# Another order for the first batch of a packed-attention and gated-FFN kernel, with the two elementwise steps of softmax 2 swapped between VectorE and GpSimd

## The chip, the core and the metric

The kernel runs on one core of one Trainium2 chip. The metric is device time in microseconds of one execution. A core has TensorE (PE in the profile; its weight loads stand apart as PEld), VectorE (DVE), ScalarE (ACT), GpSimd (POOL) and SyncE (SP), which issues every load and store of this kernel. Each engine runs its own list of instructions strictly in the order written, and waits where a semaphore tells it to.

## What is computed

The reference is attention of a small packed set of queries, attention of the full queries on its result, and a gated feed-forward net without a nonlinearity:

```python
def sm_attn(qq, kk, vv):
    s = scale * np.matmul(qq, kk.transpose(0, 1, 3, 2))
    s = s - np.max(s, axis=-1, keepdims=True)
    a = np.exp(s)
    a = a / (np.sum(a, axis=-1, keepdims=True) + 1e-09)
    return np.matmul(a, vv)
p_packed = sm_attn(p, k, v)             # p: 8 x 8 heads x 32 x 64; k, v: 8 x 8 x 576 x 64
out = sm_attn(q, p_packed, p_packed)    # softmax 2: rows of 32
x = out as (8 * 576) tokens x 512
y = ((x @ w_a) * (x @ w_b)) @ w_out     # w_a, w_b: 512 x 1536, w_out: 1536 x 512
```

The three weight matrices arrive in 64-bit floating point, everything else in 32 bits. The output is float32.

## The kernel before

The work goes batch by batch (`for b in range(B)`, 8 batches of 576 tokens and 8 heads). The heads are split in two halves, e = 0 and e = 1, four heads each.

**Attention of a batch.** `stage1(b, e)` makes the packed attention of one half: scores (L247), maximum (L253), exponential on ScalarE (L257), transposes on TensorE (L271, L272), product with v (L281), and the scaled result `pp` (L287). `turned` turns `pp` into `ppT` (L236, L237). `stage2(b, e)` is the second attention: scores (L297), then softmax 2 on a tile `s2`: a transpose to 32-wide rows (L302), maximum (L304), subtraction of the maximum (L307), exponential (L309), sum and reciprocal (L312 to L314), multiplication by the reciprocal (L315), a transpose back (L318), and a split into a rounded high part `a2_hi` (L319, ScalarE) and a low part `a2_lo` (L322, which the profile shows at the helper's line L86). L307 and L315 run on the engine that the variable `eng` holds. In the profile `s2` of batch 0 is called s, later ones t, and the parts a_hi and a_lo.

**FFN of a batch.** The second attention's product with the packed values is not formed by itself: `g_tiles(b, c)` multiplies `ppT` with a 512-wide piece of `w_ab` (L332), and `mm1` multiplies that with the softmax parts. `g_tiles` also splits its result into `ghi` (ScalarE, L338) and `glo` (VectorE, shown at L86). One call serves two of the twelve steps `ft` of `mm1`. A step makes two products with three passes each (high with high, high with low, low with high), 12 matmuls of 288 columns a half (L351): the first goes into one pair of PSUM banks (`pa`), ScalarE copies it to `asb` (L363), the second goes into the other pair (`pb`), and VectorE multiplies the two (L366). There are two pairs: the next step's first product waits for L363, its second for L366. ScalarE and GpSimd then split the gated result into `h_hi` (L370) and `h_lo` (L86). After twelve steps `mm2_part` (L377) multiplies with `wo_hi` and `wo_lo`, three passes again. For batch 0 it goes through the first nine slices of `w_out` for all four token tiles, one slice after the other, so that slices can be converted late.

**Weight conversion**, in batch 0 alone. 36 pieces of 512 KB are loaded (`raw`, 12 buffers) and turned into 32 bits by three steps, each run in order of the pieces: A (`high_word`, ScalarE, L189), B (`low_word`, on ScalarE at L197, or on VectorE or GpSimd at L194, as the table `WAYS` says with 0, 1 or 2), and C (`both_words`, VectorE, L200), after which the buffer is free and the next piece is loaded. Pieces 4c to 4c + 3 are what `g_tiles` needs for c; pieces 24 to 35 are `w_out`, and for these C writes a single buffer, `wo_f32`, which step D (`split_wout`) rounds on ScalarE (L225) and subtracts on GpSimd (L86, tile wo).

**What sets the order.** All five engines follow the written order (`manual_schedule`). Three tables of short names write it for batch 0: `FIRST` the loads (p, k, q, v in parts, w a weight piece; part 0 and 1 are heads 0 to 3 and 4 to 7, part 2 the last 64 tokens of all heads), `START` all steps before the first `mm1`, and `PLAN_0`, whose slots are emitted one after each half of an `mm1` step and between the groups of `mm2`. In them T and P are `turned`, k and q the transposes of loaded keys and queries, S0 and S1 the start of `stage1`, r its further steps for each half, s0 and s1 the steps of `stage2`, g the first `g_tiles`, L a load for a later batch, A to D conversion steps. `TURN` says which engine copies each transposed piece of batch 0 out of PSUM (0 VectorE, 1 ScalarE; five for k, five for q). `PLAN` is the same for the later batches.

Of the kernel before, what the change touches and what calls it, by code (L numbers as in the profile page):

```python
# [19 lines left out]
def tile_packed_attn_gated_ffn(  # L20
# [20 lines left out]
    nc = tc.nc  # L41
    B, H, S, D = q.shape
# [42 lines left out]
    def lo_part(dst, src, hi, eng=nc.vector):  # L85
        return eng.tensor_tensor(out=dst, in0=src, in1=hi.bitcast(F32), op=ALU.subtract)  # L86

    def bank():
        return ps_x.tile([P, 512], F32, name="x")

    def bank_pair(s=False):
        return ps_s.tile([P, 2, 512], F32, name="s") if s else ps_m.tile([P, 2, 512], F32, name="m")

    def work(b, name, shape, tag=None):
        if b == 0:
            return scratch.tile(shape, F32, name=name)
        return wk.tile(shape, F32, name=tag, bufs=2 if tag == "t1" else 1)
# [82 lines left out]
    def xT_cols(b, key, u, h, cols=slice(0, HS)):  # L180
        return xTs[b, key][h // R][64 * u:64 * u + 64, h % R, cols]
# [108 lines left out]
    def stage2(b, e):  # L290

        TU = 2 * XH
        hi, lo = (t[:, e, :].rearrange("p (x u l) -> p u x l", u=2, l=TL) for t in (a2_hi, a2_lo))
        x = bank_pair(b == 1 or e == 0)
        for r in range(R):
            for u in range(2):
                nc.tensor.matmul(  # L297
                    out=x[J * r:J * r + J, u, 0:HS], lhsT=ppT[64 * u:64 * u + 64, 1 if u ^ e else 2 * (b % 2), r, :],
                    rhs=xT_cols(b, "q", u, 2 * r + e), start=True, stop=True)
        yield  # L300
        s2 = work(b, f"s2_{e}", [P, TU, J], "t1")
        nc.vector.transpose(out=s2.rearrange("p (u x) j -> p u (x j)", u=2), in_=x[:, :, 0:HS])  # L302
        mx = sm.tile([P, TU], F32, name="mx")
        nc.vector.tensor_reduce(out=mx, in_=s2, axis=AX, op=ALU.max)  # L304
        yield
        eng = nc.gpsimd if b or e else nc.vector
        eng.tensor_tensor(out=s2, in0=s2, in1=mx.unsqueeze(2).broadcast_to([P, TU, J]), op=ALU.subtract)  # L307
        yield
        nc.scalar.activation(out=s2, in_=s2, func=AF.Exp, scale=scale)  # L309
        yield  # L310
        sum2 = sm.tile([P, TU], F32, name="sum2")
        nc.vector.tensor_reduce(out=sum2, in_=s2, axis=AX, op=ALU.add)  # L312
        nc.vector.tensor_scalar(out=sum2, in0=sum2, scalar1=1e-9, scalar2=None, op0=ALU.add)
        nc.vector.reciprocal(out=sum2, in_=sum2)  # L314
        eng.tensor_tensor(out=s2, in0=s2, in1=sum2.unsqueeze(2).broadcast_to([P, TU, J]), op=ALU.mult)  # L315
        yield
        a2f = work(b, f"a2f_{e}", [P, 2, XH, TL], "t2")
        nc.vector.transpose(out=a2f.rearrange("p u x l -> p (u x l)"), in_=s2.rearrange("p x j -> p (x j)"))  # L318
        nc.scalar.copy(out=hi, in_=a2f)  # L319
        yield  # L320
        lo_part(lo, a2f, hi)
        yield  # L322
# [97 lines left out]
    def emit(b, plan, tasks={}):  # L420

        for name in plan.split():
# [30 lines left out]
            elif what == "Lp":  # L453
# [1 line left out]

    st = {}

    FIRST = ("p0 k0 k1 k2 q2 q0 v0 q1 v1 w1 w1 w1 w1 w1 w1 w1 w1 w1 w1 w1")
    START = ("T0 k0 k4 k1 k3 k2 q0 S0 S1 r0 q1 r1 r1 r0 r0 r1 r0 q2 r1 q3 P0 q4 A s0 A B s0 s0 B s1 s0 B s1 A s1 "
             "s0 C B Lp2 A C s1 s1 B A B B C B A C A s0 s1 s0 C Lk2 C B g A Lv2 A A C A B C B s1 C B A B Lk3 C A "  # L460
             "s1")
    WAYS = ("000000022220202120112012011200110102")
    TURN = ("1001111101")

    PLAN = (" | S0 | r0 |  | r0 | r0 |  | r0 Lv1 |  | S1 | r1 | q0 Lk2 | r1 |  |  | r1 q1 Lk3 |  | r1 Lv2 |  |  | "
            "T2 P0 |  |  | s0 s0 s1 g s0 |  | s1 | Lp4 s0 s1 s1 k2 | s0 | s0 | s1 s0 | s1 Lq2 | s1 | k3 Lq3")
    PLAN = dict(enumerate(PLAN.split("|")))
    PLAN_0 = ("B | C C | C A B A | C C A B B | A C A | k0 | A | B Lq0 B B | B C A C T0 A | C Lp2 C k1 | B A A | S0 "
# [3 lines left out]
    PLAN_0 = dict(enumerate(PLAN_0.split("|")))  # L472

    pieces = [(c, n) for c in range(NC) for n in range(4)] + [(NC, f) for f in range(NFT)]
# [12 lines left out]
    def convert(x):  # L487
# [14 lines left out]
        elif x == "B":  # L502
            low_word(raw, int(WAYS[pieces.index((c, n))]))
        else:
# [17 lines left out]
    ep(tc.manual_schedule(engines={ET.PE, ET.DVE, ET.Activation, ET.Pool, ET.SP}))  # L522
    for name in FIRST.split():
        what, i = name[0], int(name[1])
# [9 lines left out]
    tasks = {"g": next_g(0)}  # L534
    emit(0, START, tasks)
    drain(tasks["g"])
# [6 lines left out]
    for b in range(B):  # L543
        plan = dict(PLAN if b else PLAN_0)
        slot, tasks = [0], {"g": next_g(b + 1)}
# [73 lines left out]
```

## Time and profile before

| | |
|---|---|
| median of 3 runs | 748.11 us (747.31 to 749.12) |
| the profiled execution: its time | 747.04 us |
| the profiled execution: first to last instruction (span) | 745.3 us |
| TensorE busy, matmuls | 719.9 us, 97% of the span |
| VectorE, ScalarE, GpSimd busy | 308.8, 281.4, 214.1 us |
| read from HBM, written | 47.97 MB, 9.44 MB |

Outside the span lie 747.04 - 745.3 = 1.7 us. A busy time is the union of an engine's instructions; where TensorE is nearly always busy, what it waits for in a stretch is told by the waits and by the distance between the starts of its matmuls.

### The profile page before, as it was taken

The page shows a single profiled execution, that of the slowest core. Times are in us where ns is not written, and L with a number is a line of the kernel's source. Part 1 is how long each engine was busy: PE and PEld are TensorE (multiplying, and loading weights), DVE is VectorE, ACT ScalarE, POOL GpSimd, SP SyncE. Part 2 cuts the span into 40 slices and gives each one's busy share as a digit, 9 for nine tenths or more (in the row PEclk, how much of TensorE's full clock was granted, in tenths as well). Part 3 has the DMA queues.
Part 4 walks back from the last instruction along what each step waited for, and adds up shares of the span by engine and source line. Part 5 has one row for each costly group of instructions (what it writes and reads, how often), then busy time and mean ns, then how long its engine had stood idle before and what let it go on. Part 6 is the DMA issues. An engine that isn't in the chain of part 4 may idle for free.

```text
span 745.3 us, 13719 instructions
## 1 busy us (share of the span) xinstructions
PE 719.9 (97%) x5844; PEld 602.9 (81%) x5844; DVE 308.8 (41%) x487; ACT 281.4 (38%) x494; POOL 214.1 (29%) x155
## 2 busy tenths in 40 slices
PE   5589899999999999999999999999999999999998
PEld 4278777888888888889788897888888888888887
DVE  2898856355303553244702446045520455123200
ACT  3777743444114531344203542055311553034300
POOL 0395754334103340133301333033400334023300
PEclk9799999999999999999999999999999999999999
DMA  8999952432510414014230242314050100100011
GB/s 255 362 255 256 284 100 54 88 67 54 92 41 24 71 43 91 30 45 90 47 74 15 55 80 47 76 33 73 24 106 29 33 1 2 43 15 1 1 29 43
DMA packets 171005, 58.30 MB, mean 78 GB/s; under 512 B 140608, under 2 KB 158784, under 8 KB 170944
## 3 DMA queue, kind: packets, MB, share of 16 engines
q1 hardware_dynamic: 170944, 57.43, 31.6%
q8 instruction: 46, 0.75, 0.4%
q14 instruction: 15, 0.12, 0.0%
HBM read 47.97 MB, written 9.44 MB: 77 GB/s over the span
## 4 chain that ended last, share of the span: by engine, by line
PE 91%; DVE 3%; DMA 1%; POOL 1%; issue 1%; ACT 1%; SPq 0%; DVEq 0%; POOLq 0%; ACTq 0%
PE m L377 40%; PE m L351 39%; PE x L332 6%; PE s L281 1%; PE s L247 1%; DVE w_ab L200 1%; PE s L297 1%; DMA kn<-in_k_dram 1%; PE s L271 1%; POOL wo L86 1%; DMA raw<-in_moe_w_b_dram 1%; DVE wo_f L200 1%; PE x L236 0%; PE m L297 0%; PE m L147 0%
## 5 line engine op out<-in xcount | busy, mean ns | idle before, releaser
L377 PE MATMUL m<-wo,h_hi 128*128 128x512 f32 (+1 forms) x888 | 268.8, 385 | 0.8 <-DVE asb L366 0.8
L86 POOL TENSOR_TENSOR h_lo<-asb,h_hi 128x576 fp32r<-128x576 f32 x96 | 138.6, 1444 | 411.5 <-ACT h_hi L370 411.3
L377 PEld LDWEIGHTS m<-wo,h_hi 128*128 128x128 f32 x888 | 164.2, 188 | 40.0 <-DVE t L302 5.0
L366 DVE TENSOR_TENSOR asb<-m,asb 128x576 f32<-128x576 f32 x96 | 72.6, 756 | 279.9 <-PE m L351 277.5
L351 PE MATMUL m<-a_hi,ghi 128*128 128x288 f32 x768 | 171.0, 304 | 2.4 <-ACT asb L363 1.7
L377 PE MATMUL m<-wo,h_lo 128*128 128x512 f32 (+1 forms) x444 | 170.4, 384 | 0.0
L351 PE MATMUL m<-a_lo,ghi 128*128 128x288 f32 x768 | 163.9, 295 | 0.9 <-DVE a_lo L86 0.9
L351 PEld LDWEIGHTS m<-a_hi,ghi 128*128 128x128 f32 x768 | 122.1, 188 | 39.7 <-issue 16.8
L351 PE MATMUL m<-a_hi,glo 128*128 128x288 f32 x768 | 133.4, 295 | 1.0 <-DVE glo L86 1.0
L351 PEld LDWEIGHTS m<-a_lo,ghi 128*128 128x128 f32 x768 | 123.5, 188 | 1.1 <-DVE a_lo L86 1.1
L370 ACT CAST h_hi<-asb 128x576 fp32r<-128x576 f32 x96 | 64.7, 674 | 143.0 <-DVE asb L366 143.0
L351 PEld LDWEIGHTS m<-a_hi,glo 128*128 128x128 f32 x768 | 112.7, 188 | 1.2 <-DVE glo L86 1.2
L377 PEld LDWEIGHTS m<-wo,h_lo 128*128 128x128 f32 x444 | 83.4, 188 | 16.7
L86 DVE TENSOR_TENSOR glo<-x,ghi 128x512 fp32r<-128x512 f32 x96 | 61.7, 684 | 52.7 <-ACT ghi L338 52.7
L363 ACT COPY asb<-m 128x576 f32<-128x576 f32 x96 | 61.6, 641 | 39.2 <-PE m L351 31.5
L332 PE MATMUL x<-w_ab,ppT 64*32 64x512 f32 x768 | 57.9, 606 | 7.9 <-DVE w_ab L200 7.9
L412 ACT COPY asb<-m 128x512 f32<-128x512 f32 x24 | 14.1, 587 | 134.2 <-PE m L377 133.4
L338 ACT CAST ghi<-x 128x512 fp32r<-128x512 f32 x96 | 51.4, 588 | 5.9 <-PE x L332 5.9
L119 DVE STREAM_TRANSPOSE xT<-nat 128x1152 f32<-128x1152 f32 x28 | 38.3, 1367 | 0.0
L412 ACT COPY wo_f<-m 128x512 f32<-128x512 f32 x11 | 6.5, 588 | 55.4 <-PE m L377 55.4
L332 PEld LDWEIGHTS x<-w_ab,ppT 64*32 64x32 f32 x768 | 13.6, 106 | 15.9 <-issue 12.3
L194 POOL TENSOR_SCALAR raw<-raw 128x512 uint32<-128x512 uint32 x11 | 23.7, 2157 | 0.9
(106 smaller groups left out, 407.2 us busy)
## 6 DMA issues: line engine op xcount, KB each, us to landing
nat<-in_k_dram SPq DMA_DIRECT2D x56, 144.0 KB
nat<-in_q_dram SPq DMA_DIRECT2D x56, 144.0 KB
vt<-in_v_dram SPq DMA_DIRECT2D x28, 256.0 KB
raw<-in_moe_w_a_dram SPq DMA_DIRECT2D x12, 512.0 KB
raw<-in_moe_w_b_dram SPq DMA_DIRECT2D x12, 512.0 KB
raw<-in_moe_w_out_dram SPq DMA_DIRECT2D x12, 512.0 KB
out_dram<-asb SPq DMA_DIRECT2D x17, 256.0 KB
out_dram<-wo_f SPq DMA_DIRECT2D x10, 256.0 KB
```

Of the source, the lines that this page charges most:

```text
L86: return eng.tensor_tensor(out=dst, in0=src, in1=hi.bitcast(F32), op=ALU.subtract)
L119: nc.vector.transpose(out=xT.rearrange("p h t -> p (h t)"), in_=t.rearrange("p h x d -> p (h x d)"))
L194: (nc.vector if way == 1 else nc.gpsimd).tensor_scalar(out=low, in0=low, scalar1=2.0 ** -29, scalar2=7.0, op0=ALU.mult, op1=ALU.min)
L200: nc.vector.scalar_tensor_tensor(out=dst.bitcast(U32), in0=raw[..., 1], scalar=3, in1=raw[..., 0], op0=ALU.logical_shift_left, op1=ALU.bit ...
L332: nc.tensor.matmul(out=gps[e][J * r:J * r + J, :], lhsT=ppT[rows, 2 * (b % 2), r, :], rhs=w_ab[rows, c, r, :], start=True, stop=True)
L338: nc.scalar.copy(out=ghi[:, e], in_=gps[e])
L351: nc.tensor.matmul(out=ps[:, half, 0:HS], lhsT=gt[:, kt, i, :], rhs=at[:, kt, HS * half:HS * half + HS], start=(n == 0 and kt == 0), stop= ...
L363: nc.scalar.copy(out=asb, in_=pa[:, :, 0:HS])
L366: nc.vector.tensor_tensor(out=asb, in0=pb[:, :, 0:HS], in1=asb, op=ALU.mult)
L370: nc.scalar.copy(out=hh, in_=flat)
L377: nc.tensor.matmul(out=o[:, cols], lhsT=ht[:, c0:c0 + P], rhs=wt[:, cols], start=(ft == 0 and n == 0), stop=(ft == NFT - 1 and n == 2))
L412: nc.scalar.copy(out=ob, in_=o)
```

## The change

`stage2` of batch 0 runs L307 and L315 of half 0 on GpSimd and those of half 1 on VectorE; before it was the other way round. The table `SUBS` has one digit for each half of batches 0 and 1; for batch 1 it says GpSimd, as before. The other tables are written anew.

```diff
-        eng = nc.gpsimd if b or e else nc.vector
+        eng = nc.vector if b < 2 and SUBS[2 * b + e] == "1" else nc.gpsimd
...
-    FIRST = ("p0 k0 k1 k2 q2 q0 v0 q1 v1 w1 w1 w1 w1 w1 w1 w1 w1 w1 w1 w1")
...
+    FIRST = ("p0 k0 k2 k1 q0 v0 q1 v1 q2 w1 w1 w1 w1 w1 w1 w1 w1 w1 w1 w1")
...
-    TURN = ("1001111101")
...
+    TURN = ("0001110101")
+    SUBS = ("0100")
```

In `WAYS` five digits change: pieces 18, 30 and 33 go from VectorE to ScalarE, piece 34 from ScalarE to VectorE, piece 35 from GpSimd to ScalarE. In `START` the last part of the queries (q4) now stands ahead of P0, and the conversion steps stand elsewhere between the steps of softmax 2. In `PLAN_0` T0, the transposes of batch 1's packed queries, stand in slot 7 and not in 8, which is half a step of `mm1` earlier; T2, the same for batch 2, in slot 21 and not in 29; the conversions keep their own order and stand in other slots.

Three places on VectorE show what the tables do to an engine's list. The first is in the middle of softmax 2 of batch 0: from the last two of the first four conversions to the first gated product (L366). In both lists two conversions stand before the first row. Before:

```order
L200 SCALAR_TENSOR_TENSOR w_ab<-raw 128x2x256 x2
L318 STREAM_TRANSPOSE a2f_405<-s_0_344 128x576
L318 STREAM_TRANSPOSE a2f_408<-s_1_361 128x576
L86 TENSOR_TENSOR a_lo<-a2f_405,a_hi 128x2x9x32
L200 SCALAR_TENSOR_TENSOR w_ab<-raw 128x2x256 x2
L86 TENSOR_TENSOR glo<-x,ghi 128x512 x2
L200 SCALAR_TENSOR_TENSOR w_ab<-raw 128x2x256 x2
L86 TENSOR_TENSOR a_lo<-a2f_408,a_hi 128x2x9x32
L200 SCALAR_TENSOR_TENSOR w_ab<-raw 128x2x256 x2
L366 TENSOR_TENSOR asb<-m,asb 128x576
```

The same engine and place in the changed kernel:

```order
L200 SCALAR_TENSOR_TENSOR w_ab<-raw 128x2x256 x2
L318 STREAM_TRANSPOSE a2f_404<-s_0_352 128x576
L318 STREAM_TRANSPOSE a2f_407<-s_1_362 128x576
L200 SCALAR_TENSOR_TENSOR w_ab<-raw 128x2x256
L86 TENSOR_TENSOR a_lo<-a2f_404,a_hi 128x2x9x32
L86 TENSOR_TENSOR glo<-x,ghi 128x512 x2
L200 SCALAR_TENSOR_TENSOR w_ab<-raw 128x2x256
L86 TENSOR_TENSOR a_lo<-a2f_407,a_hi 128x2x9x32
L200 SCALAR_TENSOR_TENSOR w_ab<-raw 128x2x256 x4
L366 TENSOR_TENSOR asb<-m,asb 128x576
```

Two of the conversions that stood ahead of a_lo of half 1 stand behind it now, ahead of the first gated product.

The second place is VectorE in the steps 7 to 9 of batch 0's `mm1`, where the first slices of `w_out` are converted (wo_f is the buffer `wo_f32`). Before:

```order
L366 TENSOR_TENSOR asb<-m,asb 128x576
L200 SCALAR_TENSOR_TENSOR w_ab<-raw 128x2x256 x2
L200 SCALAR_TENSOR_TENSOR wo_f_917<-raw 128x512
L194 TENSOR_SCALAR raw<-raw 128x512
L366 TENSOR_TENSOR asb<-m,asb 128x576
L200 SCALAR_TENSOR_TENSOR wo_f_964<-raw 128x512
L194 TENSOR_SCALAR raw<-raw 128x512
L86 TENSOR_TENSOR glo<-x,ghi 128x512 x2
```

In the changed kernel:

```order
L366 TENSOR_TENSOR asb<-m,asb 128x576
L200 SCALAR_TENSOR_TENSOR w_ab<-raw 128x2x256
L200 SCALAR_TENSOR_TENSOR wo_f_935<-raw 128x512
L194 TENSOR_SCALAR raw<-raw 128x512
L260 TENSOR_SCALAR rs<-rs 128x1
L261 RECIPROCAL rs<-rs 128x1
L366 TENSOR_TENSOR asb<-m,asb 128x576
L200 SCALAR_TENSOR_TENSOR wo_f_983<-raw 128x512
L86 TENSOR_TENSOR glo<-x,ghi 128x512 x2
```

One conversion less stands ahead of the first wo_f, and `glo` follows the second wo_f without an L194 between.

The third place is VectorE at the end of `mm1` of batch 0: the last two gated products, behind which `mm2` starts. Before:

```order
L200 SCALAR_TENSOR_TENSOR wo_f_1050<-raw 128x512
L366 TENSOR_TENSOR asb<-m,asb 128x576
L287 TENSOR_SCALAR pp<-s,rs 128x64 x2
L200 SCALAR_TENSOR_TENSOR wo_f_1127<-raw 128x512
L366 TENSOR_TENSOR asb<-m,asb 128x576
L194 TENSOR_SCALAR raw<-raw 128x512
```

In the changed kernel:

```order
L200 SCALAR_TENSOR_TENSOR wo_f_1050<-raw 128x512
L366 TENSOR_TENSOR asb<-m,asb 128x576
L287 TENSOR_SCALAR pp<-s,rs 128x64 x2
L237 COPY pT<-x 128x256
L366 TENSOR_TENSOR asb<-m,asb 128x576
L119 STREAM_TRANSPOSE xT_1147<-nat_722 128x1152
```

The fifth wo_f no longer stands ahead of the last gated product; the copy of T2 stands there.

## Rows read from the trace of the kernel before

**Rows 1.** Stretches: length, busy us of each engine, clock, DMA share, GB/s.

```profile
25.00:41.25 16.25, 5.79 (x32) 2.36 (x31) 15.93 (x26) 13.09 (x24) 9.74 (x6) 0.68 0.97 334
41.25:66.00 24.75, 24.39 (x212) 19.91 (x213) 23.64 (x33) 18.04 (x32) 18.76 (x11) 1.00 0.96 258
66.00:92.68 26.68, 24.59 (x247) 21.15 (x245) 19.93 (x30) 19.79 (x37) 17.81 (x12) 1.00 0.97 268
130.00:745.30 615.30, 612.05 (x4899) 519.42 (x4897) 218.65 (x350) 204.68 (x355) 147.63 (x108) 1.00 0.22 47
```

**Rows 2.** Waits of TensorE: us in total, times, longest.

```profile
PE m L351 <- ACT asb L363: 1.7, 2, 1.3
...
PE x L152 <- DMA kn<-in_k_dram: 1.3, 1, 1.3
...
PE m L377 <- DVE asb L366: 0.8, 1, 0.8
```

**Rows 3.** Chain that ended last, 16 to 24 us: start, us, what.

```profile
16.60 0.47 ACT xT L149
...
21.72 0.63 PE x L152 x8
...
23.61 0.80 DVE s L302
```

**Rows 4.** The same chain, 25 to 42 us.

```profile
25.22 0.76 DVE s L307
...
29.82 1.20 DVE w_ab L200 x2
...
32.20 2.10 DVE w_ab L200 x2
...
36.48 1.55 DVE w_ab L200 x2
...
39.25 1.27 DVE w_ab L200 x2
...
41.25 1.58 PE m L351 x10
```

**Rows 5.** Timeline of TensorE, first `g_tiles`: start, us, instruction, wait before.

```profile
32.89 1.93 PE L332 MATMUL x<-w_ab,ppT 64*32 64x512 f32 x8 [7.88 <-DVE w_ab L200]
```

**Rows 6.** Timeline of GpSimd, softmax 2 of batch 0.

```profile
27.54 1.16 POOL L307 TENSOR_TENSOR s<-s,mx 128x576 f32<-128x576 f32 x1 [26.24 <-DVE mx L304]
32.34 1.40 POOL L315 TENSOR_TENSOR s<-s,sum 128x576 f32<-128x576 f32 x1 [3.65 <-ACT raw L189]
```

**Rows 7.** Line L200, 22 to 95 us: duration in ns, least/median/most.

```profile
L200 DVE SCALAR_TENSOR_TENSOR w_ab<-raw x24: 628/683/1783, 29.7 to 74.1; 128x512 uint32<-128x512 uint32 x24
...
L200 DVE SCALAR_TENSOR_TENSOR wo_f<-raw x5: 889/1902/1919, 74.7 to 90.1; 128x512 uint32<-128x512 uint32 x5
```

**Rows 8.** VectorE by line, 41.25 to 66 us: busy us, mean ns, idle before.

```profile
L200 DVE SCALAR_TENSOR_TENSOR w_ab<-raw 128x512 uint32<-128x512 uint32 x13 | 10.9, 856 | 0.6 <-POOL raw L194 0.4
...
L194 DVE TENSOR_SCALAR raw<-raw 128x512 uint32<-128x512 uint32 x4 | 2.8, 729 | 0.0
```

**Rows 9.** The chain again, 42 to 61 us: the `g_tiles` of c = 1 and c = 3.

```profile
42.83 1.02 PE x L332 x16
...
59.04 1.84 PE x L332 x16
```

**Rows 10.** Timelines of ScalarE and VectorE, 78 to 92 us.

```profile
80.65 0.62 ACT L225 CAST wo<-wo_f 128x512 fp32r<-128x512 f32 x1 [1.59 <-DVE wo_f L200]
...
82.13 0.65 ACT L363 COPY asb<-m 128x576 f32<-128x576 f32 x1
...
78.71 1.90 DVE L200 SCALAR_TENSOR_TENSOR wo_f<-raw 128x512 uint32<-128x512 uint32 x1 [1.11 <-POOL wo L86]
...
90.06 1.90 DVE L200 SCALAR_TENSOR_TENSOR wo_f<-raw 128x512 uint32<-128x512 uint32 x1 [1.02 <-POOL wo L86]
```

**Rows 11.** Waits of SyncE's queue, 0 to 60 us.

```profile
SPq L210 <- DVE w_ab L200: 10.4, 4, 6.7
```

More of the change, by code (lines that the diff above doesn't have):

```diff
@@ L456, in tile_packed_attn_gated_ffn @@
     st = {}
-    FIRST = ("p0 k0 k1 k2 q2 q0 v0 q1 v1 w1 w1 w1 w1 w1 w1 w1 w1 w1 w1 w1")
[L459 to L462, printed above, removed]
-    TURN = ("1001111101")
+    FIRST = ("p0 k0 k2 k1 q0 v0 q1 v1 q2 w1 w1 w1 w1 w1 w1 w1 w1 w1 w1 w1")
+    START = ("T0 k0 k4 k1 k3 k2 q0 S0 S1 r0 r1 q1 r1 r0 r0 r1 r0 q2 r1 q3 q4 P0 s0 B s1 A s0 B A A s0 s0 B s1 C A "
+             "s1 B s0 C s1 A s1 C B B Lp2 C A B A s0 s1 B C B B s0 B g A C A A s1 Lv2 Lk2 C C A A C B B Lk3 C s1")
+    WAYS = ("000000022220202120012012011200010010")
+    TURN = ("0001110101")
+    SUBS = ("0100")
     PLAN = (" | S0 | r0 |  | r0 | r0 |  | r0 Lv1 |  | S1 | r1 | q0 Lk2 | r1 |  |  | r1 q1 Lk3 |  | r1 Lv2 |  |  | "
@@ L467, in tile_packed_attn_gated_ffn @@
     PLAN = dict(enumerate(PLAN.split("|")))
-    PLAN_0 = ("B | C C | C A B A | C C A B B | A C A | k0 | A | B Lq0 B B | B C A C T0 A | C Lp2 C k1 | B A A | S0 "
[3 rows of a table removed]
+    PLAN_0 = ("A | C C | B A B A | B C C B C | A A | C | B | C B A T0 k0 Lp2 A | A A B B C Lq0 | C C k1 | A B A | "
[3 rows of a table added]
     PLAN_0 = dict(enumerate(PLAN_0.split("|")))
```

6 rows, old and new, of the table PLAN_0 are left out of this document.

## The prediction

> **What bounds the kernel now.** I read the stretches first [rows 1]. From 130 us on TensorE is busy for 612.05 of 615.30 us at the full clock, and the rest is the last copy and store: that part moves as a block, and what batch 0 ends earlier or later is what the kernel gains or loses. Nothing of the change lies behind batch 0's mm2. So I ask only where TensorE stands before its first L377.
>
> There are two such parts. From 25 to 41.25 us it is busy for 5.79 of 16.25 us, at a mean clock of 0.68, while VectorE is busy for 15.93 [rows 1]: the chain runs through VectorE's queue, from softmax 2 (L302, 23.61) to the a_lo of half 1, behind which the second part of the first mm1 step starts at 41.25 [rows 3, 4]. These 17.64 us are VectorE's list, one instruction behind the other. From 41.25 to the first L377 TensorE is nearly full, with three waits: two for L363, 1.3 the longest of 1.7 in all, and 0.8 for L366 at the start of mm2 [rows 2]. A fourth is hidden in a busy row: the g_tiles of c = 3 holds the chain for 1.84 us, that of c = 1 for 1.02 [rows 9].
>
> **The change, part by part.**
>
> *Loads of batch 0, up to softmax 2.* The transposes of k stop for 1.3 us until the third part of k lands, which was loaded behind the second [rows 2]. Now it is loaded ahead of it; together the parts are as large as before, so the second lands when the third did. The transposes of the third fill that wait, and scores and first maximum come 1.3 us earlier. I take 1.2, because part of this work then runs while the clock is still low. Less if another load is late: bound 0 to 1.5. Behind that, two edits cancel by my reading: a copy of q leaves ScalarE ahead of half 1's exponential, -0.47, and the eight transposes of q4 now stand ahead of P0, on the path to ppT, +0.63, of which the copy of q3 on VectorE, which waits there anyway, hides a little [rows 3]. Softmax 2 thus starts at 23.61 - 1.2 = 22.4. **-1.2.**
>
> *Softmax 2, the engines swapped.* VectorE has as many subtractions and products as before, for the other half. On GpSimd they take 1.16 and 1.40 [rows 6], on VectorE 0.76 the subtraction, and I take the same for the product [rows 4]: 1.0 longer for half 0. I cost this at nothing: while GpSimd works, VectorE does the transpose and maximum of half 1, a conversion and its subtraction, and later half 1's sums and product; the transpose back of half 0 (L318) stands behind all that. Without this cover it costs up to 1.0.
>
> *VectorE's list from 22.4 on.* In before, eight conversions (L200) stand ahead of a_lo of half 1, in four pairs of 1.20, 2.10, 1.55 and 1.27 [rows 4]; now six. The two that go are half of the last two pairs: (1.55 + 1.27) / 2 = 1.4. The second pair is 0.9 longer than the first; the trace shows GpSimd's L315 from 32.34 on beside it [rows 4, 6]. Now L315 starts before that pair, beside one conversion and sums, and I take the 0.9 as gone. Against this, VectorE will reach glo before ghi is there. The first g_tiles starts behind the third conversion, and ahead of that stand the same steps in both lists: at 32.89 - 23.61 = 9.3 us into the list, at most a little earlier. Its first eight matmuls take 1.93 at the low clock [rows 5], all sixteen, overlapped, some 3.5; with the cast (0.6) ghi of half 0 is there at 13.4. VectorE ends the fourth conversion at 34.30 - 23.61 - 0.9 = 9.8; two transposes (1.5), a conversion (0.6) and a_lo of half 0 (0.7) later it is ready, at 12.6. So it waits 0.8. Sum -1.4 - 0.9 + 0.8 = **-1.5**, and the mm1 run that started at 41.25 starts at 41.25 - 1.2 - 1.5 = 38.55. Bounds: -0.6 (the 0.9 is only moved) to -2.3 (no wait for ghi).
>
> *What moves into the next stretch.* From 41.25 to 66 VectorE is busy for 23.64 of 24.75 us [rows 1]. The two conversions come back here, 2 x 0.683 [rows 7], less one low-word step of 0.73 that WAYS and the later slots take out of it [rows 8]: +0.6. The copy for T0, which held up the g_tiles of c = 3 by 1.84 - 1.02 = 0.8 [rows 9], now stands behind fewer conversions on VectorE, and T0 half a step earlier on TensorE: -0.8. **-0.2.** Bounds: -1.0 to +1.4. GpSimd starts on its low words about 4 us earlier, since its L315 no longer comes at 32.34, and the SP queue gets buffers back earlier: 10.4 us of its waits up to 60 us are for L200 [rows 11]. So I see no new wait for a piece.
>
> *The w_out conversions.* The 1.3 wait comes from a ping-pong over one buffer: L200 into wo_f takes a median of 1.90, against 0.68 for the same work into w_ab [rows 7]; L225 waits 1.59 for it, the casts of ghi and the copy L363 stand behind L225 on ScalarE, and the copy comes at 82.13 [rows 10]. In the new list the first wo_f stands one conversion earlier and starts before that step's h_lo on GpSimd, so that the second wo_f starts in a pause of GpSimd. By the rows laid end to end from 38.55 on, L363 comes only some 0.2 us before TensorE needs it, so I count on it, with a rival below: **-1.3**, bound 0 to -1.5. At the end of mm1 the last L366 stood behind a wo_f of 1.90 (90.06) [rows 10]; now a copy of T2 stands there, ready long before: **-0.8**, bound 0 to -0.9.
>
> The narrow rows are the ones where a VectorE instruction runs beside GpSimd: 1.78 against 0.68, 1.90 against 0.68 [rows 7]. The Trainium skill (SBUF — State Buffer, Who interferes with whom) states a lock: a VectorE instruction with two SBUF inputs and a GpSimd one that reads SBUF exclude each other, and the one that starts second waits until the first has ended. The rows agree, with up to 1.2 us a time. By this rule the gain of the wo_f part hangs on who starts first, which is the second rival below.
>
> Sum: -1.2 - 1.5 - 0.2 - 1.3 - 0.8 = -5.0. The profiled execution took 747.04, so 742.0; it lies 1.07 below the median of the runs, 748.11, to which I hold the forecast: **743.1 us**.
>
> **Rivals.**
>
> *The list of VectorE becomes the bound, and it is slower.* Place: 38 to 62 us, where VectorE has two conversions more, TensorE comes earlier, and GpSimd is busy for 18.76 of 24.75 [rows 1]. For it: 95% busy before, and a conversion there took 0.856 on average, 0.17 over its median [rows 7, 8]. Against it: L366 has most of a half step of slack, and GpSimd's low words come earlier. Price: 14 conversions stand there; at m us each they add 14 x (m - 0.856). The gain of 5.0 is used up at m = 1.21, and at 1.35, if nearly all stand behind a GpSimd instruction, the time is 748.1 - 5.0 + 6.9 = 750.0. Chance 0.08.
>
> *The waits on the w_out side stay.* The lock falls the other way, the ping-pong over wo_f keeps its pace, and the 1.3 and 0.8 are paid again: 743.1 + 2.1 = 745.2. For it: the margin of 0.2, and five wo_f of which the median is a blocked one [rows 7]. Against it: one conversion less in front, and no wo_f at all ahead of the last L366. Chance 0.22.
>
> *The loads bind, and there is little or no change.* The DMA share is 0.96 to 0.97 from 25 to 92.68 [rows 1]. If pieces land when they did, what TensorE gains at the start it waits for later, and only the two waits of the first part of mm1 and a little of the start remain: 748.1 - 1.0 = 747.1. Against it: 10.4 us of SP's waits are for buffers, not for landings [rows 11], and no row of TensorE's waits behind the first 10 us names a load [rows 2]. Chance 0.11.
>
> **How the numbers follow.** The forecast's own case, all five terms within their bounds and not all at one end, has 0.59 and reaches from 741.1 to 745. With the second rival (about 744 to 746.5) and most of the third this gives a range of 741.1 to 747.4, which leaves out the slower rival, the end of the third and the best ends of the terms. A change of 0.2%, 1.5 us, is about what a measurement of this kernel tells from none. Faster by more than that (below 746.6): 0.59 + 0.22 + a small part of the third, 0.81; within: 0.10; slower (above 749.6): 0.09, the first rival and some that I did not think of.
>
> **What would show it.** Right: the first L302 near 22.4, and the second part of the first mm1 step near 38.6; the wait of L152 for k gone; the g_tiles of c = 3 as short as the others; no wait of TensorE over 0.5 us between 60 us and the first L377, which comes some 4 us earlier, and behind it no 0.8; everything from batch 1 on the same, some 5 us earlier. Wrong: waits of L351 for L366 or glo between 38 and 62 us with conversions of over 1 us in front of them (first rival); L225 waiting over 1 us ahead of ghi near 75 us (second); L351, L332 or VectorE waiting for raw or nat (third). The clock is a common risk: if it comes back later than 37 us, the first products run at half speed, and 0.1 us a matmul is lost for as long.

## The result, and the profile after

The changed kernel takes 741.73 us (median of 4 runs, 740.84 to 741.94), the kernel before 747.93 us beside it (4 runs): a ratio of 0.9913, 95% interval 0.9896 to 0.9930, so 6.2 us less where 5.0 were forecast. Of the two profiled executions, on which the forecast was built, the span falls from 745.3 to 740.2 us, by 5.1.

First the stretches of the changed kernel (columns as in [rows 1]): to the g_tiles of c = 1, from there to 66 us, to the first L377, and the rest.

```profile
25.00:41.11 16.11, 8.12 (x48) 5.95 (x55) 15.84 (x26) 13.02 (x23) 12.88 (x7) 0.58 0.99 345
41.11:66.00 24.89, 24.89 (x234) 20.54 (x234) 21.83 (x33) 20.07 (x36) 17.17 (x11) 1.00 1.02 277
66.00:86.39 20.39, 20.39 (x220) 18.61 (x213) 15.96 (x27) 16.84 (x30) 16.22 (x11) 1.00 0.98 266
125.00:740.20 615.20, 611.95 (x4898) 519.35 (x4896) 219.27 (x350) 204.56 (x355) 147.57 (x108) 1.00 0.22 47
```

These are not quite the cuts of [rows 1]: there 41.25 lies inside the first step of `mm1`, and 92.68 is the fourth L377. To the g_tiles of c = 1, the first stretch of before is:

```profile
25.00:42.76 17.76, 7.30 (x42) 3.71 (x41) 17.44 (x27) 13.86 (x26) 11.25 (x6) 0.71 0.98 321
```

The last row of the changed kernel is that of before: the rest moved as a block. In its two middle rows TensorE never stands. In the first it is busy longer than before, 8.12 against 7.30 us, at a lower mean clock, 0.58 against 0.71. Its waits, that answer to [rows 2]:

```profile
PE x L332 <- DVE w_ab L200: 8.1, 1, 8.1
...
PE x L147 <- DMA kn<-in_k_dram: 2.9, 1, 2.9
...
PE m L351 <- ACT ghi L338: 0.7, 1, 0.7
...
PE s L281 <- DMA vt<-in_v_dram: 0.3, 1, 0.3
```

The waits for L363 and L366 are gone, and that of L152 for the third part of k; so are two of before that stood inside the first step of `mm1`:

```profile
PE m L351 <- DVE glo L86: 1.0, 1, 1.0
PE m L351 <- DVE a_lo L86: 0.9, 1, 0.9
```

One is longer: the first L147 waits 2.9 for the first part of k, 1.6 before. One is new, for vt, the loaded v of batch 1, in the first part of `mm2`. The chain, at the places of [rows 3, 4, 9] (the chain counts a group from the end of what stood before it, so it starts up to 0.1 later than in a timeline):

```profile
23.17 0.80 DVE s L302
...
32.30 2.51 PE x L332 x16
35.43 5.68 PE m L351 x24
41.11 1.02 PE x L332 x16
...
56.73 1.02 PE x L332 x16
```

L302 comes 0.44 earlier, not 1.2. From 35.43 to 41.11 the chain runs through TensorE and no longer through VectorE's list. The timeline of TensorE shows why that step is so long:

```profile
35.43 0.85 PE L351 MATMUL m<-a_hi,ghi 128*128 128x288 f32 x2 [0.69 <-ACT ghi L338]
...
39.44 0.68 PE L351 MATMUL m<-a_hi,glo 128*128 128x288 f32 x2
...
40.69 0.42 PE L351 MATMUL m<-a_hi,glo 128*128 128x288 f32 x2
...
78.22 0.42 PE L351 MATMUL m<-a_hi,ghi 128*128 128x288 f32 x2
```

Two matmuls take 0.68 until 40.4 and 0.42 behind it: by stretches of 0.25 us the granted clock is 0.50 (1.2 GHz) from 26.8 to 40.4, and 1.00 (2.4 GHz) after. In before it was back at 37.0. (The last row, at 78.22, is for the w_out part further down.) VectorE, at the places of [rows 4, 10], was done earlier:

```profile
34.60 0.74 DVE L86 TENSOR_TENSOR a_lo<-a2f,a_hi 128x576 fp32r<-128x576 f32 x1
35.41 1.29 DVE L86 TENSOR_TENSOR glo<-x,ghi 128x512 fp32r<-128x512 f32 x2
...
37.22 0.75 DVE L86 TENSOR_TENSOR a_lo<-a2f,a_hi 128x576 fp32r<-128x576 f32 x1
...
45.61 0.76 DVE L366 TENSOR_TENSOR asb<-m,asb 128x576 f32<-128x576 f32 x1 [1.12 <-PE m L351]
...
70.94 0.69 DVE L200 SCALAR_TENSOR_TENSOR wo_f<-raw 128x512 uint32<-128x512 uint32 x1
...
74.50 0.73 DVE L200 SCALAR_TENSOR_TENSOR wo_f<-raw 128x512 uint32<-128x512 uint32 x1 [0.34 <-POOL wo L86]
```

The a_lo of half 1 is ready at 37.97, 14.80 us behind the first L302; in before it took 17.58. VectorE then waits for TensorE (1.12), and the first two wo_f take 0.69 and 0.73 where they took 1.92 and 1.90.

### The profile page after: what moved, and what is told of

Its sections match the earlier page's. It is cut to its first block, busy times and chain, and to the rows that moved or that the text cites. A ratio compares the mean times of both kernels' runs of the same rounds, so it can differ in the third digit from the quotient of the medians.

```text
span 740.2 us, 13720 instructions
## 1 busy us (share of the span) xinstructions
PE 719.2 (97%) x5844; PEld 605.0 (82%) x5844; DVE 304.4 (41%) x487; ACT 282.7 (38%) x495; POOL 211.8 (29%) x154
## 4 chain that ended last, share of the span: by engine, by line
PE 95%; DVE 1%; DMA 1%; SPq 1%; ACT 0%; issue 0%; DVEq 0%; ACTq 0%
PE m L351 43%; PE m L377 39%; PE x L332 7%; PE s L281 1%; PE s L247 1%; PE s L297 1%; PE s L271 1%; DMA kn<-in_k_dram 1%; DMA vt<-in_v_dram 1%; PE x L236 0%; PE m L297 0%; PE m L147 0%; PE x L147 0%; SPq L177 0%; DVE w_ab L200 0%
## 5 line engine op out<-in xcount | busy, mean ns | idle before, releaser
L377 PE MATMUL m<-wo,h_hi 128*128 128x512 f32 (+1 forms) x888 | 268.7, 385 | 0.0
L377 PEld LDWEIGHTS m<-wo,h_hi 128*128 128x128 f32 x888 | 164.2, 188 | 38.8 <-DVE t L302 5.0
L366 DVE TENSOR_TENSOR asb<-m,asb 128x576 f32<-128x576 f32 x96 | 72.7, 757 | 281.2 <-PE m L351 279.1
L351 PE MATMUL m<-a_hi,ghi 128*128 128x288 f32 x768 | 171.6, 305 | 0.7 <-ACT ghi L338 0.7
L377 PE MATMUL m<-wo,h_lo 128*128 128x512 f32 (+1 forms) x444 | 170.4, 384 | 0.0
L351 PE MATMUL m<-a_lo,ghi 128*128 128x288 f32 x768 | 164.7, 296 | 0.0
L351 PEld LDWEIGHTS m<-a_hi,ghi 128*128 128x128 f32 x768 | 123.2, 190 | 37.3 <-issue 15.9
L351 PE MATMUL m<-a_hi,glo 128*128 128x288 f32 x768 | 134.1, 296 | 0.0
L351 PEld LDWEIGHTS m<-a_lo,ghi 128*128 128x128 f32 x768 | 124.3, 190 | 0.0
L351 PEld LDWEIGHTS m<-a_hi,glo 128*128 128x128 f32 x768 | 113.5, 190 | 0.0
L377 PEld LDWEIGHTS m<-wo,h_lo 128*128 128x128 f32 x444 | 83.4, 188 | 16.7
L363 ACT COPY asb<-m 128x576 f32<-128x576 f32 x96 | 61.6, 641 | 37.5 <-PE m L351 29.8
L332 PE MATMUL x<-w_ab,ppT 64*32 64x512 f32 x768 | 56.1, 606 | 8.1 <-DVE w_ab L200 8.1
L332 PEld LDWEIGHTS x<-w_ab,ppT 64*32 64x32 f32 x768 | 13.5, 106 | 14.4 <-issue 12.5
L315 POOL TENSOR_TENSOR t<-t,sum 128x576 f32<-128x576 f32 x14 | 16.5, 1178 | 24.9 <-DVE sum L314 22.9
```

What stands on the lines that cost most here:

```text
L332: nc.tensor.matmul(out=gps[e][J * r:J * r + J, :], lhsT=ppT[rows, 2 * (b % 2), r, :], rhs=w_ab[rows, c, r, :], start=True, stop=True)
L351: nc.tensor.matmul(out=ps[:, half, 0:HS], lhsT=gt[:, kt, i, :], rhs=at[:, kt, HS * half:HS * half + HS], start=(n == 0 and kt == 0), stop= ...
L363: nc.scalar.copy(out=asb, in_=pa[:, :, 0:HS])
L366: nc.vector.tensor_tensor(out=asb, in0=pb[:, :, 0:HS], in1=asb, op=ALU.mult)
L377: nc.tensor.matmul(out=o[:, cols], lhsT=ht[:, c0:c0 + P], rhs=wt[:, cols], start=(ft == 0 and n == 0), stop=(ft == NFT - 1 and n == 2))
```

## The experiments

Their profiles differ first in when the loads land and when the clock comes back, so the table has the marks by which stages are compared. Starts are from the timelines, "list" runs from the first L302 to the end of the a_lo of half 1, "c = 1" from the first L302 to the second g_tiles; the last column is the stretch at a granted clock of 0.50.

| kernel | ratio to before, 95% interval | first L147 | first L302 | list | c = 1 | slow clock |
|---|---|---|---|---|---|---|
| before | | 6.87 | 23.61 | 17.58 | 19.15 | 26.8 to 37.0 |
| changed | 0.9913 (0.9896, 0.9930) | 7.90 | 23.17 | 14.80 | 17.87 | 26.8 to 40.4 |
| e9: changed again | 0.9907 (0.9892, 0.9922) | 8.52 | 23.79 | 14.79 | 17.67 | 27.0 to 40.6 |
| e1: matmuls added | 0.9892 (0.9876, 0.9908) | 7.91 | 23.51 | 14.73 | 16.29 | none |
| e2: list of eight | 0.9929 (0.9917, 0.9942) | 7.76 | 23.56 | 16.45 | 19.20 | 28.3 to 45.3 |
| e12: both of these | 0.9913 (0.9899, 0.9927) | 7.10 | 22.39 | 16.37 | 18.19 | 40.0 to 43.4 |
| e10: before, matmuls added | 1.0002 (0.9992, 1.0012) | 6.75 | 24.21 | 17.58 | 19.51 | 39.2 to 42.6 |
| e3: first loads as before | 0.9916 (0.9902, 0.9929) | 7.08 | 24.00 | 14.80 | 17.92 | 27.7 to 41.4 |
| e4: third part of k first | 0.9888 (0.9874, 0.9901) | 7.48 | 21.54 | 14.79 | 17.77 | 24.9 to 38.6 |
| e11: e1 and e4 | 0.9886 (0.9871, 0.9901) | 7.83 | 22.42 | 14.72 | 16.29 | none |
| e5: engines swapped back | 0.9917 (0.9904, 0.9929) | 7.43 | 23.09 | 15.67 | 18.70 | 27.5 to 41.1 |
| e6: T0 later | 0.9924 (0.9911, 0.9937) | 7.64 | 23.44 | 14.79 | 18.31 | 28.2 to 41.8 |
| e7: wo_f as before | 0.9920 (0.9907, 0.9933) | 7.12 | 22.76 | 14.78 | 18.20 | 27.1 to 40.8 |
| e8: wo_f ahead of the last L366 | 0.9909 (0.9896, 0.9921) | 7.23 | 23.12 | 14.80 | 17.11 | 28.5 to 38.7 |

Seven of these profiles (changed, e9, e3, e4, e6, e7, e8) run the same instructions from L302 to c = 1, and the list is the same to 0.02. Yet "c = 1" goes from 17.11 to 18.31; it is shortest in e8, where the slow stretch lasts 10.2 us and not 13.7 as in the other six. The first L147 moves by 1.4 us between kernels with the same first loads. The intervals of all variants of the changed kernel overlap with that of the changed kernel, so between them no total is clear of the noise. A cost is therefore read from its own stage, and each stage from one profile.

**Is it the clock now? (e1, e10)**

```diff
-"... P0 s0 B s1 A s0 ..."
+"... P0 s0 B s1 w9 A s0 ..."
+            elif what == "w":
+                x = bank()
+                for i in range(e):
+                    nc.tensor.matmul(out=x, lhsT=ident, rhs=firsts["k", 0][:, 0:2, :], start=True, stop=True)
```

> The changed kernel with nine matmuls of 128x512 added, whose result nobody reads, on TensorE between the second L297 and the first L332, where it stands for 8.1 us. Theory A (the clock is what the first mm1 step waits for now): the granted clock stays at 1.00 through 32 to 40 us; the first g_tiles takes 1.0 instead of 2.5 and the first step's 24 matmuls some 3.5 to 4 instead of 5.68, now with a short wait for the a_lo of half 1 (ready at 37.97 in the changed kernel); c = 1 starts at 39.2 to 39.7 instead of 41.11, and the time falls by 1.0 to 1.9 against the changed kernel, to 739.8 to 740.7. Theory B (VectorE's list is still the bound, as my prediction had it): TensorE waits for a_lo and L366 as long as it saves, c = 1 starts at 41 as before, change within 0.4. Theory C: the added work delays the first L332 behind 32.30 or costs clock later: slower.

740.64 us against 748.44 of before (changed: 741.73 against 747.93). The timeline of TensorE in e1:

```profile
24.38 7.99 PE L458 MATMUL x<-kn,ident 128*128 128x512 f32 x18
32.66 1.57 PE L332 MATMUL x<-w_ab,ppT 64*32 64x512 f32 x16 [0.28 <-DVE w_ab L200]
35.70 0.53 PE L351 MATMUL m<-a_hi,ghi 128*128 128x288 f32 x2 [1.47 <-ACT ghi L338]
...
38.30 0.54 PE L351 MATMUL m<-a_lo,ghi 128*128 128x288 f32 x2 [0.27 <-DVE a_lo L86]
```

The clock stays at 1.00, c = 1 comes 16.29 behind L302, where the seven profiles of this order have 17.11 to 18.31, and the list is within 0.1 the same. Theory A by the stage (the median alone, 1.1 below that of the changed kernel, would not show it), with three additions: the first g_tiles takes 1.57 and not 1.0, behind it TensorE waits 1.47 for ghi, since ScalarE casts a_hi (L319) first, and 0.67 is given back up to c = 2 (8.26 against 7.59). The same edit in the kernel before (there behind the second L297):

> The kernel before, with nine matmuls of 128x512 added on TensorE between the second L297 and the first L332, whose result nobody reads. Theory A (in the kernel before VectorE's list was what the first mm1 step waited for, its a_lo of half 1 ready at 41.19 whatever the clock does): the clock stays up, TensorE waits longer for glo and a_lo, c = 1 starts at 42.4 to 42.9 as before, and the time is within 0.4 of the kernel before. Theory B (the clock was part of the bound in before too): c = 1 at 41.5 or earlier, 1.0 or more faster.

749.33 us, a ratio of 1.0002, with nothing gained from L302 to c = 1 (19.51 against 19.15). The waits of its TensorE:

```profile
PE m L351 <- ACT ghi L338: 1.5, 1, 1.5
PE m L351 <- DVE glo L86: 1.1, 1, 1.1
...
PE x L332 <- DVE w_ab L200: 0.4, 1, 0.4
```

Theory A again: what TensorE saves it waits for VectorE's list, 17.58 long as before. Only its first condition failed: the clock did not stay up, it fell at 39.2, in the second of the two waits for ghi and glo, and was back at 42.6. The list bound the kernel before. In the changed one the first step is bound by the clock, and with the clock up the list is the bound again, by the 0.27 that L351 waits for a_lo in e1.

**What is a conversion in the list worth? (e2, e12)**

```diff
-"g A C A A s1 Lv2 Lk2 C C A A C ..."
+"g A C A A C C s1 Lv2 Lk2 A A C ..."
```

> The changed kernel with two conversions (L200) moved back ahead of the a_lo of half 1, so that eight stand there as in the kernel before; everything else stays. Theory A (the slow clock covers part of the list: a_lo of half 1 was ready at 37.97 and TensorE needed it at about 38.8): 1.3 us more in the list show as a wait of L351 for a_lo of 0.3 to 0.6, and the time rises by 0.3 to 0.6 against the changed kernel. Theory B (the list is the bound, my prediction's term of 1.4): c = 1 starts 1.3 to 1.4 later than 41.11 and the time rises by 1.3 to 1.4. Theory C: the step starts later in the slow stretch and the clock comes back at the same moment, so that nothing is lost: within 0.2.

743.85 us, dearer than any of the theories had it. The list grows by 1.65, of which 1.3 are the two conversions and the rest, by the chain, their wait for L189. TensorE in e2:

```profile
40.06 0.85 PE L351 MATMUL m<-a_lo,ghi 128*128 128x288 f32 x2 [0.52 <-DVE a_lo L86]
...
42.76 1.96 PE L332 MATMUL x<-w_ab,ppT 64*32 64x512 f32 x16
```

The wait for a_lo is the 0.3 to 0.6 of theory A. But the clock comes back at 45.3 only: c = 1 comes 1.33 later behind L302, its g_tiles takes 1.96 instead of 1.09, and c = 2 comes 8.78 behind c = 1 instead of 7.59. The cost, 1.6 to 2.3 us (4.6 below before, where the changed kernel is 6.2 and in e9 6.9 below), is list and clock together. With the added matmuls:

> The changed kernel with the nine added matmuls and with two conversions moved back ahead of the a_lo of half 1. Beside the changed kernel, the one with the two conversions alone (743.85, its slow clock lasting to 45.25) and the one with the matmuls alone (740.64). Theory A (two conversions cost their 1.3 in the list, and the rest of what they cost at the slow clock was its later return): the wait of L351 for a_lo grows to 1.4 to 1.7, c = 1 at 41.0 to 41.3, time 741.6 to 742.3. Theory B (what they cost is a later conversion of the pieces for c = 1 and c = 2, not the clock): over 743.

742.15 us, in the band of theory A, but not by its reason alone: L351 waits 1.92 for a_lo, the clock falls at 40.0, 1.2 behind that wait, and the g_tiles of c = 1 takes 1.96 again. So the slower clock came behind a wait of TensorE here too, and the two costs were not separated.

**The first loads (e3, e4)**

```diff
-    FIRST = ("p0 k0 k2 k1 q0 v0 q1 v1 q2 ...")
+    FIRST = ("p0 k0 k1 k2 q2 q0 v0 q1 v1 ...")
```

> The changed kernel with the order of the first loads as in the kernel before (the third part of k behind the second, the third part of q ahead of v). Theory A (the trace after: the wait only went from L152 to the first L147, since the first part of k lands 1.0 later when the third is loaded beside it): the first L147 is at 6.9 again, L152 waits 1.2 to 1.4 for kn, the first L302 comes 0.0 to 0.4 later than 23.17, and the time is within 0.5 of the changed kernel. Theory B (my prediction: the third part in second place is worth 1.2): the first L302 comes at 24.2 to 24.4 and the time rises by about 1.2.

The waits of TensorE in e3:

```profile
PE x L147 <- DMA kn<-in_k_dram: 1.9, 1, 1.9
PE x L152 <- DMA kn<-in_k_dram: 1.6, 1, 1.6
```

742.60 us, L147 at 7.08 and L302 at 24.00: theory A by the time and the L147, theory B closer by the L302 (0.83 later than in the changed profile). Over all profiles both are half right. With the old order the first L147 is at 6.75 to 7.08 and L302 16.7 to 17.5 behind it (before, e3, e10, of which e3 alone has the changed START); with the new one at 7.10 to 8.52 and 15.3 to 15.9 behind it (nine profiles). The means are 6.90 and 17.04 against 7.62 and 15.58: the wait of L152 is worth 1.46 (1.34 by e3 alone), the later first part takes 0.72 back, and 0.7 remains. With three profiles on one side and a spread of 1.4 on the other, the 0.72 is a rough size. The rate of the loads bears on where it comes from (the last two columns are the DMA share and GB/s). Stretches of before:

```profile
6.00:7.00 1.00, 0.13 (x1) 0.13 (x2) 0.00 (x0) 0.00 (x0) 0.00 (x0) 1.00 1.08 381
...
8.00:9.00 1.00, 0.00 (x0) 0.00 (x0) 0.00 (x0) 0.59 (x1) 0.00 (x0) 1.00 1.05 205
```

Of the changed kernel:

```profile
6.00:7.00 1.00, 0.00 (x0) 0.00 (x0) 0.00 (x0) 0.00 (x0) 0.00 (x0) 1.00 1.17 281
...
8.00:9.00 1.00, 1.00 (x5) 0.67 (x5) 0.00 (x0) 0.00 (x0) 0.00 (x0) 1.00 1.09 341
```

The DMA engines are full in all four, yet one moves 381 GB/s and another 205. The poor stretch lies at 8 us in before, where the third part of k is awaited, and ahead of the first L147 in the changed kernel. In e3, with the old order again, the stretch from 8 to 9 us has 201 GB/s. That it is the third part that loads poorly is my reading; no run measured it alone.

```diff
-    FIRST = ("p0 k0 k2 k1 ...
-    START = ("T0 k0 k4 k1 k3 k2 ...
+    FIRST = ("p0 k2 k0 k1 ...
+    START = ("T0 k4 k0 k1 k3 k2 ...
```

> The changed kernel with the third part of k loaded ahead of the first, and transposed first. Theory A (from 7.90 on TensorE is packed, so the start hangs on when the first part of k is there; the third is a quarter as large and lands early): its eight transposes (1.0) run before the first part lands, the block of transposes ends 0.7 to 1.0 earlier, the first L302 comes at 22.2 to 22.6, and the time falls by 0.4 to 0.9. Theory B: the first part lands later by as much, or the second part or q becomes the wait: L302 within 0.2 of 23.17, time within 0.3.

740.19 us, 8.2 below before, and L302 at 21.54: theory A, with more gain than it had, as far as the medians tell. In the chain of e4 all transposes of k stand in a row behind one landing, the eight of the third part being done before:

```profile
3.27 4.08 DMA kn<-in_k_dram
...
7.48 1.94 PE x L147 x8
9.42 1.71 PE m L147 x8
```

**The engine swap (e5)**

```diff
-    SUBS = ("0100")
+    SUBS = ("1000")
```

> The changed kernel with the engines of softmax 2 as in the kernel before (half 0 on VectorE, half 1 on GpSimd), the order unchanged. Theory A (my prediction: the swap itself costs and gives nothing, since other work covers it): the first L332 within 0.4 of 32.30, time within 0.4 of the changed kernel. Theory B (the swap is what keeps GpSimd's product clear of VectorE's conversions): the product on GpSimd meets conversions again, one or two L200 take over 1.2, the a_lo of half 1 comes 0.9 or more later than 37.97, and the time rises by 0.3 to 0.9. Theory C (the longer steps of GpSimd on half 0 did cost): up to 1.0 faster.

742.27 us, 6.2 below before, so 0 to 0.7 more than the changed kernel, and a list longer by 0.87. GpSimd's product and VectorE's pair of conversions in e5:

```profile
31.60 1.40 POOL L315 TENSOR_TENSOR s<-s,sum 128x576 f32<-128x576 f32 x1 [3.05 <-ACT raw L189]
```

```profile
31.37 2.19 DVE L200 SCALAR_TENSOR_TENSOR w_ab<-raw 128x512 uint32<-128x512 uint32 x2
```

The pair takes 2.19 as in [rows 4], against 1.28 in the changed kernel, whose L315 runs at 28.81: theory B in its mechanism, and in its price by the list. The time, at 0 to 0.7, does not tell it from theory A.

**T0 (e6)**

```diff
-"... C B A T0 k0 Lp2 A | A A B B C Lq0 ..."
+"... C B A k0 A | A A B B C T0 Lp2 Lq0 ..."
```

> The changed kernel with T0 (the transposes of p for batch 1 and the copy L237) moved back by one half step, behind the conversions that stand there, as in the kernel before. Theory A (my prediction's 0.8: the copy holds a bank that the g_tiles of c = 3 needs): this g_tiles takes 1.6 to 1.9 in the chain instead of 1.02, and everything behind it comes 0.6 to 0.9 later; at the end 0.1 to 0.9 is left, since a new wait for vt of 0.7 in the first part of mm2 can swallow it. Theory B (it was the conversions for c = 3, blocked beside GpSimd, that held it up, and not T0): 1.02 as in the changed kernel, time within 0.3.

743.48 us, 5.0 below before. TensorE at c = 3 in e6:

```profile
57.60 1.04 PE L332 MATMUL x<-w_ab,ppT 64*32 64x512 f32 x2
58.86 1.09 PE L332 MATMUL x<-w_ab,ppT 64*32 64x512 f32 x14 [0.22 <-DVE pT L237]
```

Fourteen of the sixteen matmuls wait for the copy L237. From c = 3 to c = 4 it takes 9.69 instead of 8.43: theory A, with 1.26 where it had 0.6 to 0.9. In before the same copy ends at 59.74, and the g_tiles of c = 3 takes 1.91 from 58.97 on.

**The wo_f conversions (e7, e8)**

```diff
-"... B A r0 | C C C | B A Lq1 |  | C C B r0 r0 D A A ..."
+"... B A r0 | C C | B A Lq1 | C C C | B r0 r0 D A A ..."
```

> The changed kernel with one w_ab conversion and the first wo_f conversion one step earlier and later so that the first two wo_f stand in the steps where they stood in the kernel before. Theory A (my prediction: it is the place of the first wo_f against h_lo on GpSimd that makes the ping-pong): an L200 into wo_f takes 1.9 again, L225 waits over 1.0, L363 of that step comes late and L351 waits 0.8 to 1.4 for it; up to that much slower, less 0.7 that the wait for vt can swallow. Theory B (the 0.7 that L363 has to spare in the changed kernel is enough in either order): no wait of L351 over 0.3, time within 0.4.

742.52 us; from c = 5 to the first L377 13.71 instead of 12.66, so 1.05 more. VectorE, ScalarE and TensorE in e7:

```profile
71.48 1.92 DVE L200 SCALAR_TENSOR_TENSOR wo_f<-raw 128x512 uint32<-128x512 uint32 x1
...
73.43 0.62 ACT L225 CAST wo<-wo_f 128x512 fp32r<-128x512 f32 x1 [0.97 <-DVE wo_f L200]
...
77.72 0.65 ACT L363 COPY asb<-m 128x576 f32<-128x576 f32 x1
...
80.81 0.54 PE L351 MATMUL m<-a_hi,ghi 128*128 128x288 f32 x2 [0.53 <-DVE asb L366]
```

The first wo_f takes 1.92 again, L225 waits 0.97 for it, the casts of ghi come 0.97 later (76.77 against 75.80), and with them L363 and glo. L351 waits 0.13 for L363 and 0.53 for an L366 that stands behind glo; by the starts of its matmuls these places cost 0.28 and 0.76. Theory A in place and price, but most of the wait is for L366 and not for L363. The span hides most of it (740.4): its loads landed earlier (L302 at 22.76), and the wait for vt is not there.

```diff
-"| r0 T2 |  | q0 B r1 C B D r1 C ..."
+"| r0 T2 | B C | q0 r1 B D r1 C ..."
```

> The changed kernel with one conversion into wo_f moved ahead of the last L366 of mm1, as in the kernel before. Theory A (my prediction's 0.8): it is blocked beside GpSimd and takes 1.9, the last L366 comes 0.5 to 0.9 later, L377 waits 0.5 to 0.9 for it; at the end 0 to 0.9, since the wait for vt behind it can swallow up to 0.7. Theory B (the conversion has the 1.58 us in which VectorE stands idle ahead of this L366): no wait of L377, time within 0.3.

741.56 us, no more than the changed kernel. Its profile has the wait:

```profile
PE m L377 <- DVE asb L366: 0.6, 1, 0.6
```

From the first L377 to the fourth it takes 1.53 instead of 0.79. The mechanism is there, with 0.74. That the time does not show it is in line with the early return of the clock in this profile (38.7, with c = 1 0.76 nearer to L302 than in the changed kernel). Its other runs have no profile, but their mean granted clock is 0.992 to 0.993, as in the profiled one (0.992), against 0.991 in three of the four runs of the changed kernel: the clock seems to have come back early in all of them. Why it did is open.

**What repeats, and both gains together (e9, e11)**

> The changed kernel itself once more, as the base for the others of this call. Theory A (the wait for vt of 0.7 in the first part of mm2 and the hour at which the clock comes back differ from one execution to the next): no wait of L281 for vt this time, as in the eight other profiles; from the fall of the clock to its return 10 or 13.5 to 14 us; the first part of k lands between 6.9 and 7.9; span 738.5 to 740.5, median within 0.7 of 741.7. Theory B (the wait for vt belongs to this order): 0.5 to 0.8 again.

742.10 us. The wait for vt is gone, as in all other profiles: theory A. Instead batch 1's k landed late, at 61.0; L247 waits for it, and c = 3 to c = 4 takes 9.39 instead of 8.43. Here theory A was not wide enough: the span is 741.0, the first part of k landed at 8.5.

> The changed kernel with both edits that were faster alone: the third part of k loaded and transposed first, and nine matmuls that keep TensorE busy ahead of the first g_tiles. Theory A (the two gains add up, since one lies ahead of softmax 2 and the other behind it): first L302 at 21.3 to 21.9, c = 1 at 37.7 to 38.3, time 738.0 to 739.2. Theory B (the weight pieces for c = 2 land when they did, near 40 us in the kernel with the added matmuls alone, and become the wait): c = 1 as in A, but c = 2 not before 46.5 to 47, waits of VectorE for raw of over 1 us, and the time 739.4 to 740.4, no better than the third part of k first alone.

740.20 us, no better than e4: theory B in the time. The gain of the clock is there (16.29 from L302 to c = 1), but the loads landed late in this profile (L302 at 22.42), and behind c = 1 the chain goes through a weight piece:

```profile
33.77 5.55 DMA raw<-in_moe_w_b_dram
39.33 1.15 DVE w_ab L200
40.47 0.68 DVE asb L366
```

c = 2 comes 8.09 behind c = 1, against 7.60 in e4, and at 46.80 against 46.91. VectorE's waits for raw of over 1 us, that theory B expected, are not there. So the pieces take 0.49 of the 1.48 that the clock gives. The rest went to loads in this profile: 0.88 to the later L302, and 0.45 between c = 3 and c = 4 (8.88 against 8.43), where VectorE waits for batch 1's k and the L247 that use it take 1.17 instead of 0.72; 0.31 comes back between c = 2 and c = 3. At c = 4 both stand at 63.5. Whether e11's other runs lost it in the same places is open. e4, the smaller edit, is the version to keep: 740.19 us. Its interval overlaps with those of the changed kernel, so the profile has to speak for it: L302 at 21.54 and in e11 at 22.42, against 22.39 to 23.79, 23.20 on average, in the nine profiles with the third part in second place. WAYS, TURN and the move of q4 had no run of their own.

## Why the prediction was right, step by step

| step, by its marks | forecast | profile, before to after |
|---|---|---|
| to the first L302 | -1.2 | 23.61 to 23.17: -0.44 |
| L302 to c = 1 (VectorE's list) | -1.5 | 19.15 to 17.87: -1.28 |
| c = 1 to c = 4 (what moves on, T0) | -0.2 | 25.47 to 24.05: -1.42 |
| c = 4 to the first L377 (w_out) | -1.3 | 22.74 to 21.30: -1.44 |
| first to fourth L377 (last L366) | -0.8 | 1.71 to 0.79: -0.92 |
| fourth L377 to batch 1's first g_tiles | 0 | 33.44 to 33.84: +0.40 |
| sum | -5.0 | -5.10 |

That the sum was right in the two profiles is in part luck: the loads (0.76) and the list (0.22) were forecast too large and the 0.40 in `mm2` was not foreseen, and this met 1.22 that the third term lacked and 0.26 in the two terms on w_out. In the 0.40 is the wait for vt: in e9, the same kernel without it, the stretch takes 33.10, 0.34 less than before. The medians differ by 6.2; the extra 1.1 is that before's profiled execution was 0.9 below its median and the changed one's 0.2 above.

**Loads: mis-sized.** The wait of L152 went, and the distance from L147 to L302 fell by 1.46 on average. The step that failed is "scores and first maximum come 1.3 us earlier": the prediction asked when the second and the third part land, and left the first, loaded beside the third, where it was. It landed 1.03 later in this profile, 0.7 on average. The reason for taking 1.2 and not 1.3, a clock still low, stands in no row: the granted clock reads 1.00 from 5 to 20 us in before, though four transposes take 1.11 at 10.26 and 0.66 at 15.18.

**The list: the mechanism right, the size too small, and only part of it in the time.** The list fell by 2.78, more than the bound of -2.3. Taken back one by one, the two conversions are worth 1.65 (e2) and the swap 0.87 (e5). The 0.9 of the blocked pair was right, but it hangs on the swap: the prediction costed the swap at nothing and put the 0.9 under the list, where L315 "starts before that pair"; with the new order and the engines swapped back, L315 starts in the pair again. The Trainium skill (SBUF — State Buffer, Who interferes with whom) says of such a pair that the second starter waits; the trace agrees, with 2.19 against 1.28. The 0.8 for ghi did not come: VectorE reaches glo at 35.34, the first half of ghi is there at 35.38, since the sixteen matmuls took 2.44 and not 3.5.

Of the 2.78 the time got 1.28 up to c = 1, because the common risk that the prediction named last came true: the clock came back at 40.4 and not at 37.0, and the first step ran at half speed. By the prediction's own mark, the run of matmuls that started at 41.25 starts at 38.96 (38.55 was forecast), 15.79 behind L302 and not 17.64; up to c = 1 it then takes 2.08 where it took 1.51. e10 shows that the step waited for the list in before, and e1 that it waits for the clock now: with the clock up, c = 1 comes 16.29 behind L302, which is the whole gain of the list. That -1.28 lies near -1.5 is luck: a list term too small met a cost of the clock that the sum did not have.

**The next stretch: short by 1.2.** T0 gave its 0.8 (9.26 to 8.43 from c = 3 to c = 4), and e6 shows that T0 is the cause. The two returned conversions, priced at +0.6, cost nothing: VectorE had waits of 1.12 and 0.63 there, and its conversions from 41 to 66 us took 0.92 on average, far from the 1.21 that would have used up the gain, so the first rival (its list as the bound) had no ground. And the smaller wait for L363 (0.36 at 55.38 in before) went too, which the sum had left out: from c = 2 to c = 3 it takes 8.03 instead of 8.62.

**w_out: right.** The first wo_f starts 0.3 before h_lo, the second in a pause of GpSimd, L225 waits 0.40, and L363 ends at 77.52, 0.7 ahead of the L351 at 78.22 that needs its bank; the margin of 0.2 was too careful. e7 puts the first wo_f back and gets 1.05 of wait. The last L366 gave 0.92, and e8 brings 0.74 back. So the second rival fell, and the third too in this profile: no landing held TensorE in `mm1`. But the third is not without ground: in e9, the same kernel, batch 1's k held it up by 0.96, and in this profile vt cost 0.7 in `mm2`. Which load is late differs from one execution to the next. ScalarE in the changed kernel:

```profile
75.27 0.62 ACT L225 CAST wo<-wo_f 128x512 fp32r<-128x512 f32 x1 [0.40 <-DVE wo_f L200]
...
76.87 0.65 ACT L363 COPY asb<-m 128x576 f32<-128x576 f32 x1
```

## What to carry to other kernels

When an engine that was waited for becomes faster, look at the clock of the engine that waited: here VectorE's list became 2.8 us shorter and TensorE used 1.3 of it, because the clock came back 3.4 us later and the first step ran at half speed. A load moved ahead of another need not be free for the ones beside it (here the first part came 0.7 later on average): follow the first landing as well as the one that was waited for. And when executions differ by up to 1.4 us in a landing and by 3.5 in how long the clock is low (10.2 and 13.7), compare stages by their own marks; totals hide a cost of 0.7.

## What the runs showed of the hardware

The clock came back 4.1 us behind the start of TensorE's first g_tiles in before, 8.1 in the changed kernel, 6.5 in e8 and 12.6 in e2; between e8 and the changed kernel no instruction ahead of it differs. In the changed kernel TensorE worked without a gap from 35.43 on and still ran at the low clock until 40.4. The fall came 1.8 (before) to 4.4 us (e8) behind the end of L297, and in e10 and e12 the clock fell in or behind waits of 1.1 to 1.9 us. Nine matmuls whose result nobody reads (18 records, 7.99 us) held it up in e1 and e11, and cost nothing in that stretch, since TensorE stood there anyway: the first L332 still waits 0.28 for w_ab behind them in e1.
